# Threshold attention with a feed-forward block: fewer weight conversions in the first slots, w_ch2 by 128 output columns, diagonals on ScalarE

## The chip, the core and the metric

The kernel runs on one core of a Trainium2 chip. The core has five engines that run their own instruction streams in order: TensorE (PE, matrix products; PEld are its weight loads), VectorE (DVE), ScalarE (ACT), GpSimd (POOL) and SyncE (SP, which here only issues transfers). They meet through semaphores. The metric is the device time of one execution in microseconds: before the change 1488.72 us, the median of three runs (1486.18 to 1491.72).

## The reference, cut to what matters

Attention keeps, in each row of scores, only those within tau of the row's maximum. Its output, with the heads side by side, goes through a normalised two-layer block with a residual.

```python
# q, k, v: (8, 8, 576, 64) float32, tau = 0.02
scores = np.matmul(q, k.transpose(0, 1, 3, 2)) / 8
thresh = np.max(scores, axis=-1, keepdims=True) - tau
scores = np.where(scores >= thresh, scores, -1e9)
attn = np.exp(scores - np.max(scores, axis=-1, keepdims=True))
attn = attn / (np.sum(attn, axis=-1, keepdims=True) + 1e-9)
x = np.matmul(attn, v).transpose(0, 2, 1, 3).reshape(8, 576, 512)

xn = (x - mean(x)) / np.sqrt(var(x) + 1e-6) * g_ln          # over the last axis
out = x + np.maximum(xn @ w_ch1, 0) @ w_ch2                 # 512x2048, 2048x512
```

The two weight matrices arrive as 64-bit floats, 8 MB each. [...]the kernel turns their bits into float32 itself.

## The kernel before, in words

**Slots.** The 8 batches have 8 heads each; a unit is one pair of heads of one batch. For each batch the kernel runs nine slots: four with the first 256 query rows of each unit, one (s = 4) that gathers what the blocks of 32 rows leave over of all four units, and four with the next 256 rows. A slot makes 2304 columns of scores (L359, or L344 in the fifth slot), takes each row's maximum (`neg`, L372, two instructions on DVE), exponentials on ACT (`e`, L383, four), and the threshold with the row sum (L390, four on DVE, then a reciprocal, L394). There is one set of score banks: the next slot's scores wait until L390 of this slot has read them. A unit's q and k must have been turned by DVE (`kT` L304, `qT` L313, `q_diag` L316) after POOL has scaled q (L301); the buffers of q and k are single, so the loads of the next unit (L112) wait for those transposes.

**Turning the attention weights.** In the first batch PE does it: `tp` and `tr` (L100, L443) multiply the weights by a diagonal matrix that holds the reciprocals, so that turning and dividing are one product. The diagonals (`diag`, L404, four a slot) are made by POOL from an identity. ACT copies `tp` to `em` (L437) and `tr` to `rest` (L452), and the products with v (`pv`, L511) run in the next slot. From the second batch on POOL divides and a transpose on DVE and a trip through DRAM turn the weights.

**Feed-forward.** After the fifth and the ninth slot of a batch 288 rows of x are complete (a group g). POOL adds the four parts of x (`sum`, L537), PE averages over the features (`mean`, L546), DVE centres (`xc`, L552), and `ffn_steps` (L605) hands out the products one by one: sixteen blocks `p1` over w_ch1, each with a ReLU copy into `hidden` on ACT (L622), then four blocks `p2` over w_ch2, each of sixteen products. `second_part` (L675) puts some of these products into each quarter of a slot, as many as a pace (`owed`) asks for, so that PE has work while the softmax chain runs. `ready` (L668) gives the quarter in which a group starts: 24 (slot 6) for the first, 41 for the second. PE's order is thus fixed when the program is written out; the engines then only wait for each other. `ps_ff` has two PSUM buffers, shared by `tp`, `tr`, `mean`, `p1` and `p2`.

**Weights.** The class `Weights` (L160) brings the 16 chunks of w_ch1 and 16 of w_ch2 in, 128 partitions by 512 numbers each. A chunk takes raw space and, while it is converted, made space; both come from a list of pieces (`free`) in memory that is not in use yet: parts of `w2_sb`, of `hidden`, of the buffer `et`, and `stage`. A tick does up to three things, for three different chunks: `end` (L260: DVE L266 finishes the number and, for w_ch1, POOL L271 multiplies by g_ln), `carry` (L253: an integer add on POOL, L257), `begin` (L229: L239 and L243 on DVE, L247 and L251 on ACT). Which ticks a slot has stands in the main loop:

```python
ticks = range(1, 4 + n // 3) if n < 6 else range(6)
```

so three in slots 0 to 2, four in slots 3 to 5, six from slot 6 on. `fetch` (L209) issues loads of further chunks on SP's queue. A chunk of w_ch2 is 128 rows by all 512 columns, so that the first block `p2`, which needs all 2048 rows, needs all sixteen chunks; `ffn_steps` hands out no product whose chunk isn't converted in program order (L639).

Of the kernel before, what the change touches and what calls it, by code (L numbers as in the profile page):

```python
# [8 lines left out]
F32 = mybir.dt.float32  # L9
U32 = mybir.dt.uint32  # L10
I32 = mybir.dt.int32
I64 = mybir.dt.int64
# [6 lines left out]
def kernel(  # L19
# [31 lines left out]
    nc = tc.nc  # L51
    B, H, S, D = q.shape
    DM = H * D
# [3 lines left out]
    NK = DM // 128  # L57
    ND = DF // 128
    J = 4
    NB = S // 32  # L60
    TOK = S // 2
# [7 lines left out]
    consts = ctx.enter_context(tc.tile_pool(name="consts", bufs=1))  # L69
# [4 lines left out]
    ffn = ctx.enter_context(tc.tile_pool(name="ffn", bufs=2))  # L74
# [8 lines left out]
    ident = consts.tile([128, 128], F32, name="ident")  # L83
    avg_sb = consts.tile([128, 128], F32, name="avg_sb")
    w1_sb = [consts.tile([128, DF], F32, name=f"w1_{i}") for i in range(NK)]
    w2_sb = consts.tile([128, ND, DM], F32, name="w2")
    q_diag = [consts.tile([128, 128], F32, name=f"q_diag{i}") for i in range(HP)]
    rests = [consts.tile([128, 4, 128], F32, name=f"rest{i}") for i in range(2)]
    v_rest = [consts.tile([128, 2, D], F32, name=f"v_rest{i}") for i in range(HP)]
    hidden = consts.tile([128, ND, TOK], F32, name="hidden")  # L90
# [11 lines left out]
    def load_qk(u, engines=None):  # L102


        b, hp = units[u]
        tiles = []
        for i, (name, src) in enumerate((("q", q), ("k", k))):
            t = ins.tile([128, NB, 32], F32, tag=name, bufs=1, name=f"{name}_in")
            for h in range(2):
                for e in range(2):  # L110
                    g = 2 * h + e
                    (engines[i] if engines else nc.sync).dma_start(  # L112
                        out=t[32 * g : 32 * g + 32],
                        in_=src[b, 2 * hp + h, :, 32 * e : 32 * e + 32].rearrange(
                            "(n r) c -> r n c", r=32
                        ),
                    )
            tiles.append(t)
        loaded[u] = tuple(tiles)

    def load_v(u):
# [13 lines left out]
        out=tau_sb, in_=bass.AP(tensor=tau.tensor, offset=tau.offset, ap=[[0, 128], [1, 1]])  # L135
    )
    load_qk(0, (nc.sync, nc.scalar))
    for t in q_diag + rests + v_rest:
# [21 lines left out]
    class Weights:  # L160
# [12 lines left out]
        def __init__(self):  # L173
            self.chunks = [
                (w1_sb[i][:, c : c + WC], w_ch1[i * 128 : (i + 1) * 128, c : c + WC], i)
                for c in range(0, DF, WC)
                for i in range(NK)
            ] + [(w2_sb[:, i], w_ch2[i * 128 : (i + 1) * 128, :], None) for i in range(ND)]
            self.n1 = NK * (DF // WC)
            self.fetched = self.begun = self.carried = self.ended = 0  # L180
            self.raw, self.made, self.due, self.ticks = {}, {}, [], 2
            flat = lambda t: t.rearrange("p a b -> p (a b)")
            stage = consts.tile([128, 8, WC], F32, name="stage")
            et = att.tile([128, NB, 128], F32, tag="et", bufs=1, name="et0")

            n1 = self.n1
            self.free = []  # L190
            for t, n, before in (
                (w2_sb, ND // 2, lambda p: n1 + 2 * p),
                (hidden, 4, lambda p: 10),
                (et, 2, lambda p: 2 * n1),
                (stage, 4, lambda p: 2 * n1),
            ):
                for p in range(n):
                    self.free.append((before(p), -1, flat(t)[:, p * 2 * WC : (p + 1) * 2 * WC]))
# [10 lines left out]
        def fetch(self, most=99):  # L209

            while self.fetched < len(self.chunks) and most:
                i = self.fetched
                if sum(p[0] > i for p in self.free) <= 2:
                    break
                got = self.piece(i, 1)
                if got is None:
                    break
                most -= 1
                self.fetched += 1
                self.raw[i] = got  # L220
                nc.sync.dma_start(out=got[2].bitcast(I64), in_=self.chunks[i][1])

        def give(self, got):
            self.free.append((got[0], self.ticks, got[2]))
# [160 lines left out]
    def weights(es, thr, divide):  # L385


        den = small.tile([128, 4], F32, tag="den", name="den")
        for i in range(4):
            nc.vector.scalar_tensor_tensor(  # L390
                out=es[:, i], in0=blocks[i], scalar=thr[:, i : i + 1], in1=es[:, i],
                op0=ALU.is_ge, op1=ALU.mult, accum_out=den[:, i : i + 1],
            )
        nc.vector.reciprocal(den, den)  # L394
        diags = []
        for i in range(4):
            if divide:
                src = dst = es[:, i]
            else:
                if i % 2 == 0:  # L400
                    two = ffn.tile([128, TOK], F32, tag="o", bufs=6, name="diag")
                src, dst = ident, two[:, i % 2 * 128 : i % 2 * 128 + 128]
                diags.append(dst)
            nc.gpsimd.tensor_scalar(  # L404
                out=dst, in0=src, scalar1=den[:, i : i + 1], scalar2=1.0,
                op0=ALU.mult, op1=ALU.mult,
            )
        return diags
# [196 lines left out]
    def ffn_steps(g):  # L605

        xc = centred.pop(g)
        rb = None  # L610
        for d in range(ND):
            while conversion.ended < 4 * (d // 4 + 1):
                yield 0
            p1 = ps_ff.tile([128, TOK], F32, tag="ff", name="p1")
            for c in range(NK):
                product(
                    p1, lhsT=w1_sb[c][:, d * 128 : (d + 1) * 128], rhs=xc[:, c],
                    start=(c == 0), stop=(c == NK - 1),
                )
                if c < NK - 1:  # L620
                    yield 1
            nc.scalar.activation(hidden[:, d], p1, func=AF.Relu)  # L622
            yield 2
            if d == 1:
                sq = ffn.tile([128, NK, TOK], F32, tag="sq", bufs=1, name="sq")
                nc.scalar.activation(sq, xc, func=AF.Square)  # L626
                for c in range(1, NK):
                    nc.gpsimd.tensor_tensor(out=sq[:, 0], in0=sq[:, 0], in1=sq[:, c], op=ALU.add)  # L628
            if d == 8:
                var = ps_ff.tile([128, TOK], F32, tag="ff", name="var")  # L630
                product(var, lhsT=avg_sb, rhs=sq[:, 0], start=True, stop=True)
# [72 lines left out]

    conversion = Weights()
    if w_ch1.dtype == I64:
        conversion.fetch(5)
    else:
        for i in range(NK):
            nc.sync.dma_start(out=w1_sb[i], in_=w_ch1[i * 128 : (i + 1) * 128])  # L710
            nc.scalar.mul(w1_sb[i], w1_sb[i], g_sb[:, i : i + 1])
        for i in range(ND):
            nc.sync.dma_start(out=w2_sb[:, i], in_=w_ch2[i * 128 : (i + 1) * 128])
        conversion.begun = conversion.carried = conversion.ended = len(conversion.chunks)

    turn(0)
    load_qk(1)
    load_v(1)
    for n in range(NS):
        b, s = divmod(n, SLOTS)  # L720
        ticks = range(1, 4 + n // 3) if n < 6 else range(6)

        def tick(i):
            if i in ticks:
# [6 lines left out]
        es, thr = next(rest)  # L731
# [85 lines left out]
```

## Time and profile before

| | |
|---|---|
| time | 1488.72 us (1486.18 to 1491.72) |
| profiled span | 1486.6 us |
| PE busy | 1418.2 us, 95% |
| DVE busy | 875.1 us, 59% |
| POOL busy | 476.1 us, 32% |
| ACT busy | 402.5 us, 27% |
| products of the feed-forward (L100, `p`) | 515.0 + 513.9 us |
| scores (L359) | 159.7 us |
| diagonals and divisions (L404) | 186.5 us for the divisions of the later batches; 27.4 us for 36 diagonals |
| moved by DMA | 205 MB, 138 GB/s on average |

A row of the profile's timeline reads: start, duration, engine, line of the kernel, operation, what is written and read, shapes, how many were merged, and in brackets how long the engine was idle before and what released it. The busy tenths cut the span into forty equal slices, one digit each; PEclk is the clock that PE was granted, in tenths of its full speed. Busy time on PE is modelled, and covers matmuls that run at a low clock too, so a longer row for the same matmuls is lost time as well. A buffer's number is left out of its name: `w` stands for all parts of the weights, and memory that is lent to the conversion shows under the name of its owner (`hidden`, `et`, `stage`).

### The profile page before, as it was taken

What the parts mean: (1) busy time and instruction counts of PE and PEld (TensorE: products, weight loads), DVE (VectorE), ACT (ScalarE), POOL (GpSimd) and SP (SyncE); (2) the same over time, 40 slices, a digit from 0 to 9 for tenths busy, and PEclk for the clock granted to TensorE, in tenths of its full rate; (3) what the DMA queues carried; (4) which work ended last, traced back from release to release, by engine and by line L of the source; (5) the groups of instructions that cost most, each with busy time, mean ns of one, the idle gap of its engine ahead of it and who ended that gap; (6) DMA issues with size and microseconds to landing.
All of it is one profiled execution on the core that took longest, in us unless ns stands there. A gap on an engine that the chain in (4) does not pass through costs nothing.

```text
span 1486.6 us, 29712 instructions
## 1 busy us (share of the span) xinstructions
PE 1418.2 (95%) x12168; PEld 875.2 (59%) x12168; DVE 875.1 (59%) x1524; ACT 402.5 (27%) x766; POOL 476.1 (32%) x737
## 2 busy tenths in 40 slices
PE   4858989999999999999999999999999999999998
PEld 2646655565556555665556555665556655565654
DVE  5877737656664566556665566556665566655211
ACT  3655413222221222223131222213132221312020
POOL 3785323232332233232332323222332323332100
PEclk8879999999999999999999999999999999999999
DMA  9612237565865577455874587556775558555301
GB/s 227 169 57 89 58 87 146 144 165 135 180 158 140 135 170 169 132 145 141 184 170 132 132 168 180 141 140 152 165 165 143 146 130 186 156 140 126 90 9 16
DMA packets 460695, 205.12 MB, mean 138 GB/s; under 512 B 275024, under 2 KB 420176, under 8 KB 460560
## 3 DMA queue, kind: packets, MB, share of 16 engines
q1 hardware_dynamic: 458160, 202.93, 56.7%
q8 instruction: 95, 1.56, 0.4%
q10 hardware_dynamic: 2368, 0.30, 0.2%
q14 instruction: 40, 0.33, 0.1%
q0 software_dynamic: 32, 0.00, 0.0%
HBM read 119.41 MB, written 83.76 MB: 137 GB/s over the span
## 4 chain that ended last, share of the span: by engine, by line
PE 81%; DMA 5%; SPq 4%; DVE 4%; ACT 2%; POOL 2%; issue 1%; POOLq 0%; DVEq 0%; ACTq 0%
PE p L100 60%; PE sc L511 9%; PE sc L359 9%; DMA em<-scr 2%; SPq L112 2%; PE sc L100 2%; ACT e L383 1%; DVE e L390 1%; SPq L475 1%; DMA rest<-scr 1%; DMA scr<-et 1%; POOL diag L404 1%; PE tr L443 1%; PE mean L100 1%; DVE neg L372 1%
## 5 line engine op out<-in xcount | busy, mean ns | idle before, releaser
L100 PE MATMUL p<-xc,w 128*64 128x288 f32 x4096 | 515.0, 407 | 2.7 <-ACT hidden L622 1.9
L100 PE MATMUL p<-hidden,w 128*64 128x288 f32 x4096 | 513.9, 407 | 0.2 <-ACT rest L452 0.2
L100 PEld LDWEIGHTS p<-xc,w 128*64 128x64 f32 x4096 | 299.0, 137 | 195.2 <-ACT hidden L622 7.7
L100 PEld LDWEIGHTS p<-hidden,w 128*64 128x64 f32 x4096 | 300.2, 137 | 188.7 <-ACT rest L452 0.7
L372 DVE TENSOR_REDUCE neg<-sc 128x2 f32<-128x1152 f32 x144 | 189.4, 1352 | 261.7 <-PE sc L359 235.3
L383 ACT ACTIVATE e<-sc,neg 128x576 f32<-128x576 f32 x288 | 194.7, 742 | 316.9 <-DVE neg L372 316.8
L404 POOL TENSOR_SCALAR e<-e,den 128x576 f32<-128x576 f32 x252 | 186.5, 758 | 252.9 <-DVE den L394 252.9
L390 DVE SCALAR_TENSOR_TENSOR e<-sc,thr,e 128x576 f32<-128x576 f32 x288 | 219.6, 812 | 36.8 <-ACT e L383 36.2
L469 DVE STREAM_TRANSPOSE et<-e 128x1152 f32<-128x1152 f32 x112 | 153.4, 1375 | 76.2 <-POOL e L404 58.6
L622 ACT ACTIVATE hidden<-p 128x288 f32<-128x288 f32 x256 | 105.9, 414 | 302.2 <-PE p L100 301.2
L359 PE MATMUL sc<-kT,qT 64*128 64x64 f32 (+3 forms) x1024 | 159.7, 445 | 26.9 <-DVE e L390 16.8
L376 POOL TENSOR_SCALAR thr<-neg,low_sb 128x2 f32<-128x2 f32 x144 | 42.7, 297 | 375.0 <-DVE neg L372 370.0
L359 PEld LDWEIGHTS sc<-kT,qT 64*128 64x128 f32 x1024 | 88.8, 194 | 113.3 <-issue 81.6
L511 PE MATMUL sc<-em,v_in 128*64 128x256 f32 (+1 forms) x1408 | 131.4, 330 | 6.9 <-DMA em<-scr 3.5
L511 PEld LDWEIGHTS sc<-em,v_in 128*64 128x64 f32 x1408 | 88.1, 137 | 45.7 <-DVE et L469 9.8
L528 ACT COPY x<-sc 128x256 f32<-128x256 f32 x60 | 22.4, 373 | 308.5 <-PE sc L511 305.0
L569 DVE TENSOR_TENSOR o<-p,rb 128x288 f32<-128x288 f32 x64 | 28.5, 445 | 130.1 <-PE p L100 130.1
L570 POOL TENSOR_TENSOR o<-o,x 128x288 f32<-128x288 f32 x64 | 51.0, 797 | 129.2 <-DVE o L569 127.3
L537 POOL TENSOR_TENSOR sum<-sum,x 128x256 f32<-128x256 f32 (+1 forms) x64 | 31.9, 498 | 84.2 <-ACT x L528 81.7
L628 POOL TENSOR_TENSOR sq<-sq 128x288 f32<-128x288 f32 x48 | 38.7, 806 | 40.4 <-ACT sq L626 37.9
L511 PE MATMUL sc<-rest,v_rest 128*64 128x256 f32 (+1 forms) x352 | 44.8, 329 | 0.0
L537 POOL TENSOR_TENSOR sum<-x 128x256 f32<-128x256 f32 (+1 forms) x32 | 16.3, 508 | 72.4 <-ACT x L528 43.8
(111 smaller groups left out, 774.7 us busy)
## 6 DMA issues: line engine op xcount, KB each, us to landing
scr<-et SPq DMA_DIRECT2D x252, 288.0 KB, 4.6
em<-scr SPq DMA_DIRECT2D x63, 1024.0 KB, 5.9
q_in<-in_q_dram SPq DMA_DIRECT2D x128, 72.0 KB, 3.7
out_dram<-ot SPq DMA_DIRECT2D x256, 36.0 KB, 4.2
k_in<-in_k_dram SPq DMA_DIRECT2D x124, 72.0 KB, 2.7
v_in<-in_v_dram SPq DMA_DIRECT2D x64, 128.0 KB, 4.2
rest<-scr SPq DMA_DIRECT2D x63, 128.0 KB, 5.9
w<-in_moe_w_ch_dram SPq DMA_DIRECT2D x12, 512.0 KB, 4.8
```

The lines of the kernel that those rows point to most:

```text
L100: nc.tensor.matmul(out[r], lhsT=lhsT[:, r], rhs=rhs, **flags)
L359: nc.tensor.matmul(sc[h][:, at : at + n], lhsT=qT[r, half, j * 128 : (j + 1) * 128], rhs=kT[r, o : o + n], start=True, stop=True,)
L372: nc.vector.tensor_reduce(out=neg[:, i], in_=sc[h][:, : 2 * S].rearrange("p (j n) -> p j n", j=2), axis=AXL.X, op=ALU.max, negate=True,)
L376: nc.gpsimd.tensor_scalar(out=thr[:, i], in0=neg[:, i], scalar1=-1.0, scalar2=low_sb, op0=ALU.mult, op1=ALU.add,)
L383: nc.scalar.activation(es[:, i], blocks[i], func=AF.Exp, bias=neg[:, i : i + 1])
L390: nc.vector.scalar_tensor_tensor(out=es[:, i], in0=blocks[i], scalar=thr[:, i : i + 1], in1=es[:, i], op0=ALU.is_ge, op1=ALU.mult, accum_o ...
L404: nc.gpsimd.tensor_scalar(out=dst, in0=src, scalar1=den[:, i : i + 1], scalar2=1.0, op0=ALU.mult, op1=ALU.mult,)
L469: nc.vector.transpose(et[:, :, 64 * h : 64 * h + 64].rearrange("p n (j c) -> p j n c", j=2), es[:, 2 * h : 2 * h + 2].rearrange("p j (n c) ...
L511: nc.tensor.matmul(dst[64 * h : 64 * h + 64], lhsT=vt[:, c, h, :] if c < J else vr[:, h, :], rhs=pick(em[:, c] if c < J else er, hp, h), s ...
L537: nc.gpsimd.tensor_tensor(out=sums[g][:, cols], in0=x[:, 0, cols] if c == 1 else sums[g][:, cols], in1=x[:, c, cols], op=ALU.add,)
L570: nc.gpsimd.tensor_tensor(out=o, in0=o, in1=groups[g][:, m], op=ALU.add)
L622: nc.scalar.activation(hidden[:, d], p1, func=AF.Relu)
```

## The change

It does six things.

- The ticks of slots 0 to 2 go from three to two, and of slots 3 to 5 from four to three. Six conversions move behind slot 5, where the slots have six ticks as before.
- w_ch2 is kept as `w2_sb[128, 4, 16, 128]`, by blocks of 128 output columns. A chunk is four blocks of 128 rows by 128 columns, and the first block `p2` needs the first four chunks only, the second the next four, and so on. It is meant to let the deferred conversions arrive in time.
- The diagonals of the first batch are made by ScalarE (`nc.scalar.mul`, identity times reciprocal) and no longer by POOL.
- The q and k of the second unit are issued by ACT's queue, and no longer stand on SP's queue behind the first weight chunks. Four chunks are fetched first, not five.
- The first group starts at quarter 25 and the second at 42, one later each: its mean and centring move into slot 6 (10), behind the first `tp` products.
- The third buffer of `x`, not in use before the second batch, is lent to the conversion as one more piece (`x_room`).

```diff
-    w2_sb = consts.tile([128, ND, DM], F32, name="w2")
+    w2_sb = consts.tile([128, NK, ND, 128], F32, name="w2")
...
-            ] + [(w2_sb[:, i], w_ch2[i * 128 : (i + 1) * 128, :], None) for i in range(ND)]
+            ] + [
+                (
+                    w2_sb[:, m, d : d + 4].rearrange("p d c -> p (d c)"),
+                    w_ch2[d * 128 : (d + 4) * 128, m * 128 : (m + 1) * 128].rearrange(
+                        "(d p) c -> p d c", p=128
+                    ),
+                    None,
+                )
+                for m in range(NK)
+                for d in range(0, ND, 4)
+            ]
...
+            x_room = ffn.tile([128, NK, TOK], F32, tag="x", bufs=3, name="x_room")
...
+                (x_room, 1, lambda p: 2 * n1),
...
-            if divide:
-                src = dst = es[:, i]
-            else:
+            if not divide:
                 if i % 2 == 0:
                     two = ffn.tile([128, TOK], F32, tag="o", bufs=6, name="diag")
-                src, dst = ident, two[:, i % 2 * 128 : i % 2 * 128 + 128]
-                diags.append(dst)
+                diags.append(two[:, i % 2 * 128 : i % 2 * 128 + 128])
+                nc.scalar.mul(diags[i], ident, den[:, i : i + 1])
+                continue
             nc.gpsimd.tensor_scalar(
-                out=dst, in0=src, scalar1=den[:, i : i + 1], scalar2=1.0,
+                out=es[:, i], in0=es[:, i], scalar1=den[:, i : i + 1], scalar2=1.0,
...
-                while conversion.ended < conversion.n1 + d + 1:
+                while conversion.ended <= conversion.n1 + 4 * m + d // 4:
                     yield 0
                 product(
-                    p2, lhsT=w2_sb[:, d, m * 128 : (m + 1) * 128], rhs=hidden[:, d],
+                    p2, lhsT=w2_sb[:, m, d], rhs=hidden[:, d],
...
-            return (24, 41)[g]
+            return (25, 42)[g]
...
-        conversion.fetch(5)
+        conversion.fetch(4)
...
-    load_qk(1)
+    load_qk(1, (nc.scalar, nc.scalar))
...
-        ticks = range(1, 4 + n // 3) if n < 6 else range(6)
+        ticks = range(1, 3 + n // 3) if n < 6 else range(6)
```

More of the change, by code (lines that the diff above doesn't have):

```diff
@@ L191, in __init__ @@
             for t, n, before in (
-                (w2_sb, ND // 2, lambda p: n1 + 2 * p),
+                (w2_sb.rearrange("p m d c -> p (m d) c"), ND // 2, lambda p: n1 + 2 * p),
                 (hidden, 4, lambda p: 10),
                 (et, 2, lambda p: 2 * n1),
+                (x_room, 1, lambda p: 2 * n1),
                 (stage, 4, lambda p: 2 * n1),
@@ L220, in fetch @@
                 self.raw[i] = got
-                nc.sync.dma_start(out=got[2].bitcast(I64), in_=self.chunks[i][1])
+                _, src, gi = self.chunks[i]
+                raw = got[2].bitcast(I64)
+                nc.sync.dma_start(
+                    out=raw if gi is not None else raw.rearrange("p (d c) -> p d c", d=4), in_=src
+                )
         def give(self, got):
@@ L712 @@
         for i in range(ND):
-            nc.sync.dma_start(out=w2_sb[:, i], in_=w_ch2[i * 128 : (i + 1) * 128])
+            nc.sync.dma_start(
+                out=w2_sb[:, :, i],
+                in_=w_ch2[i * 128 : (i + 1) * 128, :].rearrange("p (m c) -> p m c", m=NK),
+            )
         conversion.begun = conversion.carried = conversion.ended = len(conversion.chunks)
     turn(0)
-    load_qk(1)
+    load_qk(1, (nc.scalar, nc.scalar))
     load_v(1)
```

## The prediction

> **What bounds the kernel now.** I read the busy tenths by slice first, then stretches, then the timelines of PE, VectorE (DVE) and GpSimd (POOL) over the first 220 us, then waits.
>
> ```profile
> PE   4858989999999999999999999999999999999998
> POOL 3785323232332233232332323222332323332100
> PEclk8879999999999999999999999999999999999999
> ```
>
> A slice is 37 us. PE is short of work, and its clock below full, only in the first four or five. The stretch from 200 us on says the rest is PE's own work:
>
> ```profile
> 200.00:1480.00 1280.00, 1271.52 (x10790) 766.71 (x10786) 732.42 (x1273) 303.98 (x590) 365.38 (x595) 1.00 0.60 142
> ```
>
> Columns: PE, weight loads, DVE, ACT, POOL busy, clock, DMA share, GB/s. PE is idle 8.5 us of 1280, at full clock; whatever comes off the start comes off the end. Summing PE over ten-microsecond stretches up to 200 gives 146.3 us busy, 53.7 idle. A slot is one unit of scores; its first row maximum on DVE (`neg`) marks it:
>
> ```profile
> 60.39 2.62 DVE L372 TENSOR_REDUCE neg<-sc 128x2 f32<-128x1152 f32 x2 [0.43 <-PE sc L359]
> ...
> 77.32 1.20 DVE L266 SCALAR_TENSOR_TENSOR hidden<-hidden 128x512 f32<-128x512 f32 x1 [2.19 <-POOL hidden L257]
> 78.44 0.41 DVE L239 TENSOR_SCALAR w<-stage 128x512 uint32<-128x512 uint32 x1
> 78.89 0.98 DVE L243 SCALAR_TENSOR_TENSOR w<-stage,w 128x512 uint32<-128x512 uint32 x1
> 79.79 2.61 DVE L372 TENSOR_REDUCE neg<-sc 128x2 f32<-128x1152 f32 x2
> ...
> 96.92 2.61 DVE L372 TENSOR_REDUCE neg<-sc 128x2 f32<-128x1152 f32 x2
> ...
> 120.04 2.61 DVE L372 TENSOR_REDUCE neg<-sc 128x2 f32<-128x1152 f32 x2
> ```
>
> Slots 0 to 6 mark at 13.86, 30.88, 44.61, 60.39, 79.79, 96.92, 120.04: pitches 17.0, 13.7, 15.8, 19.4, 17.1, 23.1. At 77 us a weight conversion stands ahead of `neg` on DVE, and waits 2.19 us for POOL, which held the diagonals:
>
> ```profile
> 71.84 3.53 POOL L404 TENSOR_SCALAR diag<-ident,den 128x128 f32<-128x128 f32 x4 [3.61 <-DVE den L394]
> 75.34 0.69 POOL L271 TENSOR_SCALAR w<-w,g_sb 128x512 f32<-128x512 f32 x1
> 76.00 1.28 POOL L257 TENSOR_TENSOR hidden<-hidden,et 128x512 int32<-128x512 int32 x1
> ```
>
> PE pays twice, in gaps and in slow matmuls after them:
>
> ```profile
> 54.87 5.89 PE L359 MATMUL sc<-kT,qT 64*128 64x512 f32 x16 [3.74 <-DVE e L390]
> ...
> 88.92 2.33 PE L359 MATMUL sc<-kT,qT 64*128 64x512 f32 x16
> ...
> 112.44 1.23 PE L100 MATMUL mean<-sum,avg_sb 128*64 128x288 f32 x4 [6.27 <-POOL sum L537]
> ...
> 123.33 0.98 PE L443 MATMUL tr<-diag,e 128*64 128x128 f32 x7 [2.63 <-ACT em L437]
> ```
>
> The same 16 score matmuls take 2.33 us, or 5.89 after a 3.74 us gap.
>
> **What the Trainium skill says.** "TensorE: Matmul & The Clock Gate", Part 1: PE falls to half clock after an idle window of about 3.4 us and needs as much busy time to return. The trace agrees: slow after gaps of 3.74, 5.45, 6.27 us, full after 2.63. "SBUF — State Buffer", Who interferes with whom: a DVE instruction with two SBUF inputs contends with a GpSimd one that reads SBUF. L266 and L243 are such, and take 0.66 to 1.2 and 0.69 to 1.8 us. "DMA: Bandwidth & Descriptors", Issuing engines are not separate DMA queues: another issuing engine saves issue time, not bandwidth; the DMA share is 0.94 to 1.15 from 0 to 20 us, so there is none spare. Price: "ScalarE: Activation LUTs", What ACT_TABLE_LOAD costs: with a per-partition pointer 280 ns + 0.833 ns an element; for 576 that is 760, and L383 measures 742.
>
> **The change, part by part.** One conversion costs DVE 0.66 + 0.42 + 0.69 = 1.8 us alone, near 2.1 beside POOL; POOL 1.3, for w_ch1 0.7 more; ACT 1.35.
>
> *One conversion fewer in each of slots 0 to 5* (9 + 12 = 21 become 6 + 9 = 15), and *diagonals on ACT*. POOL loses 3.5 + 2 us a slot: its waits on the path (2.19 before `neg`, 2.14 before a `qT` at 50.0) go. On ACT four diagonals cost between 4 x 0.27 (its 128x128 copy, L519) and 4 x 0.39 less overlap (the price): 1.1 to 1.3, I take 1.2. They stand between conversions, after the exponentials, before the next slot's `em` copies; `em` of the next slot needs its scores first, so about 0.5 us shows. Rebuilding a slot from its rows, T being `neg`:
> - Slot 1: `neg` 2.65, turn 2.0, half a conversion 1.2; the last two exponentials end at T+7.5 (as now), so `e` ends T+8.7; scores 2.3: pitch 11.1.
> - Slot 2: `neg` 2.65, turn 2.0 with 0.3 for `q_in`, conversion 2.0, `e` 3.0 to T+10; scores 2.3, over the other conversion: 12.6.
> - Slots 3 and 4, no turn: `e` ends T+9 (exponentials, 1 us wait as now), then two conversions 3.9: 12.9 each. Scores at full clock end inside that.
> - Slot 5 with slot 6's first: three conversions: 15.
>
> PE has 9.8 us in such a slot (scores 2.33, `tp` 3.85, `tr` 0.98, `pv` 2.65), with gaps of 2.0 (`pv` ends T+7.1, scores start T+9.1) to 2.2 us (round the mean, below): under the 2.63 that left it at full clock, so I take full clock.
>
> *Second unit on ACT's queue.* Now its eight loads stand on SyncE behind five weight chunks, issued 10.33 to 18.3, and DVE waits:
>
> ```profile
> 21.02 0.78 DVE L304 STREAM_TRANSPOSE kT<-k_in 128x576 f32<-128x576 f32 x1 [4.54 <-DMA k_in<-in_k_dram]
> ```
>
> ACT issued four such in 2.07 us, so eight end at 14.4 if they start at 10.33. They wait for unit 0's transposes, and behind them stand ACT's table load (1.28) and the first exponentials, which need scores at 15.2 anyway: 0.5 us later, hidden, since `e` starts only at 23.9. `kT` lands between 16.5 (DVE free) and 21.0: I take 18.0, so slot 1 at 27.9. Four chunks first instead of five helps it.
>
> *Mean one quarter later.* It no longer stalls PE 6.3 us ahead of slot 6's scores, but stands between `tp` pairs, and takes one of two PSUM buffers until DVE has centred, after `neg`. With ACT's `em` copies at 14.7 after slot 5's mark, mean to 15.9, `neg` to 17.5, centre to 19.1, `tp` and `tr`: the first w_ch1 product (`p`) starts at 21.3.
>
> Sum: 27.9 + 11.1 + 12.6 + 12.9 + 12.9 = 77.4 for slot 5, + 21.3 = 98.7. Now `p` starts at 124.04. From there PE holds a queue of products and is 93 to 100% busy to 190 us, so 25.3 us come off.
>
> *Six deferred conversions.* Slots 6 to 8 now hold 6, 6, 5. DVE: slot 8 then has 2.65 + 2.0 + 3.0 + 10 = 17.7 us, PE 9.8 + 54 products of 0.25 = 23.3: hidden. w_ch2 by output columns asks for four chunks per block of 128 instead of all sixteen, so the pause at the last product of the first block, before slot 9, goes; it cost little, since other blocks followed. Chunks land as 1 KB runs rather than 4 KB, off the path. The extra x buffer is free memory; the weight's row stride is not a cost the trace shows. Net of all these: 0, with -3 to +6 for the range.
>
> Forecast: 1488.7 - 25.3 + 0.6 for contention = 1464.
>
> **The rivals.**
> - *A, half the gain* (0.17): the second unit lands no sooner, and slots 1 to 5 lose only the DVE share of a conversion, 5 x 1.9, plus 2.5 of mean's stall: 12 us, 1476.7. For it: gaps moved by ACT's order could reach 3.7 us and halve the clock. Against: POOL's waits are measured and vanish.
> - *B, more* (0.08): slot 1 at 26.9, pitches 11.1, 12.3, 12.4, 12.4, `p` 20 on: 95, so 29, and half of the 6 us idle left between 124 and 200: 1456.7. For it: less port contention. Against: deferred conversions raise it again there.
> - *C, no gain or slower* (0.13): A's 12 us are given back by six deferred conversions at 2 us each where slot 8's products wait for them, and two restarts at half clock cost 3.5 each: 1495.7. For it: all four engines have more to do in slots 7 and 8. Against: DVE was idle 2.58 and 4.97 us around slot 8, and PE's order has 14 us of products in it.
>
> **How the numbers follow.** My forecast 0.62. Lowest: B's 1456.7 with the -3 of deferred conversions; highest: A with 2 more: 1454 to 1479 leaves C and tails out. Faster by 0.5% is below 1481.3: forecast, A and B, 0.87; C is split 0.07 same, 0.06 slower.
>
> **What would show it.** Right: marks near 28, 39, 52, 65, 77; no slow scores after slot 1; POOL never ahead of `neg`; `p` from about 99; `kT` of unit 1 near 18. Wrong: gaps over 3 us on PE between slots 1 and 5, scores of 5 us there, exponentials later than T+7.5 because of ACT's diagonals, or PE waiting for L283 (the conversion's last DVE step) in slots 8 and 9.

## The result, and the profile after

The changed kernel takes 1480.75 us (median of 4 runs, 1478.69 to 1483.58) beside 1489.39 us of the kernel before (a fourth run has joined the three behind the 1488.72): ratio 0.9945, interval 0.9919 to 0.9971. Measured once more beside other kernels (e9 below) the ratio is 0.9944, 0.9930 to 0.9957. So it is faster, by 8 us and not by 25. The profiled spans are 1479.8 and 1486.6 us.

The busy tenths of the changed kernel, slices of 37 us:

```profile
PE   2878999999999999999999999999999999999998
PEclk9999999999999999999999999999999999999999
```

The third and sixth slices are fuller (7 for 5, 9 for 8), but the first has fallen from 4 to 2: the start got worse before it got better. The 9 of TensorE's clock row in the first slice is no gain: a second profile of the same kernel (e9) has a 7 there, and the scores in this slice are slow in both (5.74 and 5.70 us for what takes 2.33). The stretch from 200 us on, columns as in the prediction:

```profile
200.00:1480.00 1280.00, 1262.61 (x10711) 766.97 (x10707) 729.14 (x1265) 303.30 (x589) 362.38 (x590) 1.00 0.59 142
```

The kernel ends 6.8 us earlier: of the 17.4 us in which PE is not busy here, 6.4 lie behind its last matmul, and 11.0 are idle where the kernel before had 8.5. The steady part is as before; the whole story is in the first 220 us. VectorE's timeline there (start, duration, what it did, idle before it):

```profile
26.19 0.78 DVE L321 STREAM_TRANSPOSE kT<-k_in 128x576 f32<-128x576 f32 x1 [9.56 <-DMA k_in<-in_k_dram]
...
69.05 0.66 DVE L283 SCALAR_TENSOR_TENSOR hidden<-hidden 128x512 f32<-128x512 f32 x1
69.63 0.42 DVE L256 TENSOR_SCALAR w<-w 128x512 uint32<-128x512 uint32 x1
70.09 1.07 DVE L260 SCALAR_TENSOR_TENSOR w<-w 128x512 uint32<-128x512 uint32 x1
71.08 1.79 DVE L283 SCALAR_TENSOR_TENSOR hidden<-hidden 128x512 f32<-128x512 f32 x1
72.79 0.95 DVE L256 TENSOR_SCALAR hidden<-w 128x512 uint32<-128x512 uint32 x1
73.77 1.06 DVE L260 SCALAR_TENSOR_TENSOR hidden<-w,hidden 128x512 uint32<-128x512 uint32 x1
74.75 2.61 DVE L389 TENSOR_REDUCE neg<-sc 128x2 f32<-128x1152 f32 x2
```

Three things are to be seen. Unit 1's `kT` waits 9.56 us for `k_in` and comes at 26.19, where it came at 21.02 before and was predicted at 18.0. In slots 1 to 5 no conversion waits 2 us for GpSimd ahead of `neg` any more (the 2.19 of before is gone; in slot 6 there is such a wait, below). But the two conversions between 69.05 and 74.75 now take 5.7 us, 2.85 each, against the 1.8 that one takes alone. GpSimd's timeline in the same microseconds shows what lies beside them:

```profile
69.83 0.78 POOL L288 TENSOR_SCALAR w<-hidden,g_sb 128x512 f32<-128x512 f32 x1 [3.99 <-DVE hidden L283]
70.59 1.73 POOL L274 TENSOR_TENSOR hidden<-hidden,w 128x512 int32<-128x512 int32 x1
```

VectorE's last step L283 (L266 in the kernel before) grew from 0.66 to 1.79 just while GpSimd's add L274 ran, and the add grew too, from 1.29 to 1.73. After it GpSimd goes on with other work up to 76 us, and VectorE's next steps are slow as well. TensorE's timeline:

```profile
30.71 5.74 PE L376 MATMUL sc<-kT,qT 64*128 64x512 f32 x16 [16.73 <-DVE e L407]
...
102.27 0.71 PE L100 MATMUL mean<-sum,avg_sb 128*64 128x288 f32 x4 [1.59 <-POOL sum L553]
...
132.26 1.75 PE L459 MATMUL tr<-diag,e 128*64 128x128 f32 x7 [3.11 <-ACT em L453]
```

The scores of slot 1 come after a gap of 16.73 us; the stall of 6.27 us ahead of the mean is down to 1.59; products start at 108.24 (124.04 before); and in slot 7 a gap of 3.11 us, not there before in this size, brings `tr` to half speed (1.75 us for 0.98).

Marks of slots, first products and the end, all in us:

| | slot 1 | slot 2 | slot 3 | slot 4 | slot 5 | first product | end of the span |
|---|---|---|---|---|---|---|---|
| before | 30.88 | 44.61 | 60.39 | 79.79 | 96.92 | 124.04 | 1486.6 |
| predicted | 27.9 | 39.0 | 51.6 | 64.5 | 77.4 | 98.7 | - |
| changed | 36.23 | 47.55 | 59.79 | 74.75 | 88.50 | 108.24 | 1479.8 |

Of the 15.8 us by which products start sooner, 6.8 are left at the end. Nine are given back, nearly all in slots 6 to 8. With the matmuls of products already issued counted at 0.125 us each (64 of them took 7.97 us; a product is two), the changed kernel leads by 16 us at the scores of slot 7, by 12 at those of slot 8, by 9 at those of slot 9, and by 8 at those of slot 16. What TensorE loses is the gaps ahead of `tr` in slots 7 and 8, 3.11 and 2.63 us, and the slow matmuls after them. VectorE in slot 6, and TensorE's scores of slot 7:

```profile
119.20 1.17 DVE L283 SCALAR_TENSOR_TENSOR w<-w 128x512 f32<-128x512 f32 x1 [2.63 <-POOL w L274]
120.30 1.52 DVE L256 TENSOR_SCALAR et<-et 128x512 uint32<-128x512 uint32 x1
121.86 1.66 DVE L260 SCALAR_TENSOR_TENSOR et<-et 128x512 uint32<-128x512 uint32 x1
...
128.98 2.62 DVE L389 TENSOR_REDUCE neg<-sc 128x2 f32<-128x1152 f32 x2
```

```profile
122.71 2.33 PE L376 MATMUL sc<-kT,qT 64*128 64x512 f32 x16
```

Five conversions run here from 112.08 to 128.98, 16.9 us in all, 3.4 each; 2.63 of the 16.9 are the wait for GpSimd's add. The third finds all three of its steps stretched, the last two only L256, from 0.42 to 1.52 (124.05 and 126.81). Two steps of the second, 1.03 and 1.18, lie beside another work of GpSimd, the squares for the variance (L644, 113.92 to 117.24). Slot 7's `neg` comes at 128.98 although its scores ended at 125.04, and slot 8's at 159.64 with scores that ended at 156.16: VectorE, not TensorE, sets the pace in slots 6 to 8.

### The profile page after: what moved, and what is told of

It is laid out like the page before. It is cut to its first block, busy times and chain, and to the rows that moved or that the text cites. A ratio compares the mean times of both kernels' runs of the same rounds, so it can differ in the third digit from the quotient of the medians.

```text
span 1479.8 us, 29677 instructions
## 1 busy us (share of the span) xinstructions
PE 1412.3 (95%) x12168; PEld 877.5 (59%) x12168; DVE 881.5 (60%) x1524; ACT 411.9 (28%) x802; POOL 455.2 (31%) x701
## 4 chain that ended last, share of the span: by engine, by line
PE 71%; DMA 7%; SPq 6%; DVE 4%; issue 2%; POOL 1%; ACT 1%; POOLq 0%; DVEq 0%; ACTq 0%
PE p L100 52%; PE sc L527 9%; PE sc L376 7%; DMA em<-scr 4%; SPq L491 2%; DMA scr<-et 2%; PE sc L100 2%; SPq L112 1%; DMA rest<-scr 1%; SPq L126 1%; SPq L130 1%; DVE e L407 1%; POOL e L420 1%; DVE neg L389 1%; ACT e L400 1%
## 5 line engine op out<-in xcount | busy, mean ns | idle before, releaser
L100 PEld LDWEIGHTS p<-hidden,w 128*64 128x64 f32 x4096 | 307.3, 137 | 181.3
L376 PE MATMUL sc<-kT,qT 64*128 64x448 f32 (+3 forms) x1024 | 158.6, 439 | 28.2 <-DVE e L407 18.7
L544 ACT COPY x<-sc 128x256 f32<-128x256 f32 x60 | 22.3, 372 | 301.2 <-PE sc L527 299.3
L644 POOL TENSOR_TENSOR sq<-sq 128x288 f32<-128x288 f32 x48 | 39.1, 814 | 39.1 <-ACT sq L642 36.6
L100 PE MATMUL tp<-diag,e 128*64 128x128 f32 x576 | 35.6, 276 | 5.9 <-ACT em L453 5.6
```

What stands on the lines that cost most here:

```text
L100: nc.tensor.matmul(out[r], lhsT=lhsT[:, r], rhs=rhs, **flags)
L376: nc.tensor.matmul(sc[h][:, at : at + n], lhsT=qT[r, half, j * 128 : (j + 1) * 128], rhs=kT[r, o : o + n], start=True, stop=True,)
```

## The experiments

My theory after the result had two parts. First, the second unit's `k` lands later on ScalarE's queue, because it is issued late there and shares the DMA engines with weight chunks. Second, with the diagonals gone GpSimd starts its add right beside VectorE's conversion steps, and both slow down. Rivals: that slot 1 is late for another reason; that conversions are long of themselves; that everything won early is taken back by slots 6 to 8 in any case. Ratios are to the kernel before; the changed kernel has 0.9944. No run undoes the layout of w_ch2, the lent buffer of `x` or the first fetch of four chunks by itself, so what these three are worth stays open.

**e1: the second unit back on SyncE.**

```diff
-    load_qk(1, (nc.scalar, nc.scalar))
+    load_qk(1)
```

> The changed kernel with the second unit's q and k issued by SyncE again (four chunks first, as changed). Theory (the move to ACT's queue is what went wrong: the next weight chunks overtook k): unit 1's kT starts near 20 to 21 us instead of 26.2, the mark of slot 1 comes at 30 to 31 instead of 36.2, all later marks move with it, and the time falls by 5 to 6 us, to about 1475. Rival (the late start is absorbed by the slots behind it, and the loss sits in slots 6 to 8 alone): the time stays within 1.5 us of the changed kernel's 1480.8.

Measured: 0.9893 (0.9877 to 0.9908), 1476.0 us; `kT` at 19.91, slot 1 marked at 29.95, 6.3 us sooner. The theory's numbers hold: this edit of the change is a loss. Of the 6.3 us, 1.9 go at once into a longer slot 1 (13.2 us to the next mark for 11.3); the lead is 4.4 at slot 6 and 4.3 at the end.

**e2: only ScalarE's queue, in the kernel before.** The same line, the other way round.

> The kernel before with only the second unit's q and k moved to ACT's queue (five chunks first, as before). Theory (the move alone costs): kT of unit 1 goes from 21.0 to 25 to 27 us, the mark of slot 1 from 30.9 to 35 to 37, and the time rises by 4 to 6 us, to about 1494. Rival (the move is harmless or of use by itself, as the prediction had it, and hurts only with the other edits): the mark at 28 to 31 and no more time than before.

Measured: 1.0033 (1.0021 to 1.0044), 5 us slower; `kT` at 27.57, and every mark from slot 1 to 9 is 6.1 to 6.2 us later. The part alone does the same harm without the rest of the change.

**e3: the diagonals back on GpSimd.**

```diff
-                nc.scalar.mul(diags[i], ident, den[:, i : i + 1])
+                nc.gpsimd.tensor_scalar(
+                    out=diags[i], in0=ident, scalar1=den[:, i : i + 1], scalar2=1.0,
+                    op0=ALU.mult, op1=ALU.mult,
+                )
```

> The changed kernel with the diagonals of the first batch made by GpSimd again. Theory (POOL's 3.5 us in a slot were on the path): slots 2 to 5 become 1 to 3 us longer each, POOL stands ahead of neg or q_in again, and the time rises by 4 to 10 us. Rival (with two and three conversions POOL has room enough, and ACT gains as much as POOL loses): slots within 0.5 us, time within 2 us of the changed kernel's.

Measured: 0.9975 (0.9962 to 0.9988), 4.6 us slower than the changed kernel. The sum was as expected and the place was not: the pitches into slots 4 and 5 are 12.75 and 12.9, *shorter* than the 15.0 and 13.75 of the changed kernel and just what the prediction had; the loss is in slots 5 to 7. VectorE and GpSimd of this kernel:

```profile
71.80 0.66 DVE L283 SCALAR_TENSOR_TENSOR hidden<-hidden 128x512 f32<-128x512 f32 x1
72.38 0.42 DVE L256 TENSOR_SCALAR w<-w 128x512 uint32<-128x512 uint32 x1
72.84 0.72 DVE L260 SCALAR_TENSOR_TENSOR w<-w 128x512 uint32<-128x512 uint32 x1
```

```profile
72.07 3.54 POOL L418 TENSOR_SCALAR diag<-ident,den 128x128 f32<-128x128 f32 x4 [2.64 <-DVE den L411]
...
76.24 1.29 POOL L274 TENSOR_TENSOR hidden<-hidden,w 128x512 int32<-128x512 int32 x1
```

With the diagonals at the head of GpSimd's queue the add comes at 76.24, when VectorE's two conversions are over, and these take 1.8 us each. The four small diagonals don't slow VectorE; it is GpSimd that pays, 3.54 us for four where another slot of this kernel has 2.48. The diagonals act as a shield. Their cost shows where a slot has more to do: slot 6 is marked 18.5 us after slot 5 (14.7 in the changed kernel).

**e4: slot 0's two weight chunks behind the second unit's loads,** ScalarE's queue kept.

```diff
-        conversion.fetch(2)
+        if n:
+            conversion.fetch(2)
         run_all(stores)
...
                 load_qk(u + 1)
+        if n == 0:
+            conversion.fetch(2)
         run_all(aside)
```

> The changed kernel, second unit on ACT's queue, but the two weight chunks that SyncE issued at 18.4 us come behind the loads of the third unit (which wait for unit 1's transposes), so none is in flight beside unit 1's k. Theory (k was late because the weights shared the transfer engines with it): k lands about 2.7 us after its last issue at 19.8, kT at 22 to 23 instead of 26.2, slot 1 at 32 to 33, 3 to 4 us off the time. Rival (k was late because ACT could not issue it before 17.8 and small packets on this queue are slow by themselves): kT stays at 25 to 26.5, the time unchanged within 1.5 us, or longer since the chunks come late.

Measured: 0.9894 (0.9880 to 0.9908), slot 1 marked at 31.67, 4.6 us sooner.

```profile
22.32 0.78 DVE L321 STREAM_TRANSPOSE kT<-k_in 128x576 f32<-128x576 f32 x1 [5.75 <-DMA k_in<-in_k_dram]
```

`k` was issued at 17.89, as late as in the changed kernel, and yet landed 3.9 us sooner. So of the late `kT`, about 4 us came from the chunks in flight beside it. The rest goes with the late issue: in e1 SyncE issued `k` from 13.54 on.

**e5: GpSimd's two steps of a conversion left out** (the weights lack the add of the low word and g_ln).

```diff
-            nc.gpsimd.tensor_tensor(out=ai, in0=ai, in1=self.words(i, I32)[:, :, 0], op=ALU.add)
...
-                out=dst if gi is None else a, in0=y, scalar=(1.0625 * 2.0**-15) ** 2, in1=a,
+                out=dst, in0=y, scalar=(1.0625 * 2.0**-15) ** 2, in1=a,
...
-            if gi is not None:
-                nc.gpsimd.tensor_scalar(
-                    out=dst, in0=a, scalar1=g_sb[:, gi : gi + 1], scalar2=1.0,
-                    op0=ALU.mult, op1=ALU.mult,
-                )
```

> The changed kernel with GpSimd's two steps of a weight conversion left out (the add of the two words, and for w_ch1 the multiplication by g_ln; VectorE's last step writes the weight straight to its place), so the weights aren't the reference's; every other instruction and every load stays. It tells whether VectorE's conversion steps are long because GpSimd works beside them. Theory (contention: with the diagonals gone from GpSimd, its add and multiplication now start together with VectorE's steps): a conversion on VectorE falls from 2.85 to about 1.9 us, slots 3 and 4 go from 15.0 and 13.75 to about 12.9, slots 6 to 8 give back 3 to 5 us less; first w_ch1 product near 104, ratio to the kernel before 0.988 to 0.991. Rival (the steps are long for another reason, such as ScalarE's or the DMA's traffic): pitches of slots 3 and 4 within 0.4 of 15.0 and 13.75, ratio 0.993 to 0.996.

Measured: 0.9831 (0.9812 to 0.9850), 17 us faster than the changed kernel, more than either theory had. VectorE:

```profile
71.42 0.69 DVE L282 SCALAR_TENSOR_TENSOR w<-hidden 128x512 f32<-128x512 f32 x1
72.02 0.42 DVE L256 TENSOR_SCALAR hidden<-w 128x512 uint32<-128x512 uint32 x1
72.48 0.69 DVE L260 SCALAR_TENSOR_TENSOR hidden<-w,hidden 128x512 uint32<-128x512 uint32 x1
...
119.83 2.62 DVE L383 TENSOR_REDUCE neg<-sc 128x2 f32<-128x1152 f32 x2 [2.93 <-PE sc L370]
```

The first three rows are the second conversion of slot 3, the same three instructions that took 3.7 us; with the one ahead of it 3.3 us instead of 5.7, and VectorE's own work is untouched. Slot 7 is marked at 119.83, and there `neg` waits 2.93 us for its scores: VectorE is no longer the bound. First product at 102.94, 5.3 us sooner; the end 16.4 us sooner. So two thirds of what GpSimd's steps cost shows only after the first product. In slots 7 and 8 TensorE's waits ahead of `tr`, 3.11 and 2.63 us in the changed kernel, are 0.28 and 0.24, and `tr` runs at full speed. The run takes GpSimd's time away as well as the contention, so 16 us is an upper bound for the latter, and no kernel that computes everything can have all of it.

**e6: the add ahead of the last step,** the same work in another order.

```diff
-            if self.ended < self.carried and self.due[self.ended] <= self.ticks:
-                self.end()
             if self.carried < self.begun:
                 self.carry()
+            if self.ended < self.carried and self.due[self.ended] <= self.ticks:
+                self.end()
```

> The changed kernel with the order inside a tick turned: GpSimd's add for the conversion begun a tick ago is issued ahead of the last step of the oldest one, so that it no longer stands behind GpSimd's multiplication by g_ln, which waits for VectorE. The work is the same. Theory (contention): the first add of a slot's two runs while VectorE waits for the exponentials (GpSimd was idle 3.99 us there), so less of it lies beside VectorE's conversion steps: slots 3 and 4 about 1 us shorter each, slots 6 to 8 1 to 2 us, ratio 0.991 to 0.993. Rival (it only moves the contention to VectorE's e steps or to the next tick): pitches within 0.4 us of the changed kernel's, ratio 0.994 to 0.996.

Measured: 0.9888 (0.9872 to 0.9904), 8 us faster than the changed kernel and more than the theory had, for two lines that change places. Pitches into slots 4 and 5 are 13.5 and 12.6; the two conversions take 4.3 us (5.7). GpSimd's first add starts before VectorE's steps do, in a gap in which it had stood idle 3.99 us.

**e7: the ticks of before,** three and four conversions a slot again.

```diff
-        ticks = range(1, 3 + n // 3) if n < 6 else range(6)
+        ticks = range(1, 4 + n // 3) if n < 6 else range(6)
```

> The changed kernel with the ticks of before: slots 0 to 5 start 3, 3, 3, 4, 4, 4 conversions and not 2, 2, 2, 3, 3, 3; all the rest of the change stays. Theory: one conversion costs a slot of 1 to 5 VectorE time of 2 to 2.9 us on the path, so the first w_ch1 product comes 9 to 12 us later, near 118; against that slots 6 to 8 hold fewer conversions and give back 5 to 8 us less; net +2 to +6, ratio 0.996 to 0.9985. Rival 1 (nothing is given back for the deferred conversions, as the prediction had it): +9 to +12, ratio 1.000 to 1.003. Rival 2 (all of it is given back): ratio 0.993 to 0.9955.

Measured: 1.0023 (1.0012 to 1.0033): 11.8 us slower than the changed kernel, and slower than the kernel before. My expectation fell. The number is that of rival 1, but not its reason: the first product comes 22.3 us later (130.5), and 8.2 us of that are won back by the end (span 1493.9), as the theory had it. What I mis-sized is a conversion in the early slots: the pitches grow by 1.9 to 6.2 us each, and in slots 4 and 5 TensorE's gaps pass 4.5 us, after which its matmuls are slow (a `tr` of 1.76 us, scores of 3.40 after it):

```profile
88.84 1.76 PE L459 MATMUL tr<-diag,e 128*64 128x128 f32 x7 [4.52 <-ACT em L453]
```

So the six deferred conversions are what makes the change faster; its other parts without them come to 3.4 us slower than before, and the move to ScalarE's queue alone cost 5 us in e2.

**e8: the mean and the products one quarter earlier again.**

```diff
-            return (25, 42)[g]
+            return (24, 41)[g]
```

> The changed kernel with the first two groups' mean and products one quarter earlier again, as before; all the rest stays. Theory (prediction's step on the mean): TensorE stalls 4 to 6 us for the sum ahead of slot 6's scores, which then also run at half clock; VectorE's centring comes earlier in exchange; slot 6's mark 3 to 6 us later, first w_ch1 product within 2 us of 108, end +1 to +4, ratio 0.995 to 0.997. Rival (VectorE bounds slots 6 to 8 anyway, so the stall is absorbed): ratio 0.994 to 0.995, lead lost at slot 6 back by slot 8.

Measured: 0.9934 (0.9915 to 0.9954), the same as the changed kernel. The stall is there, with its slow matmuls (1.23 us for four that take 0.71):

```profile
104.10 1.23 PE L100 MATMUL mean<-sum,avg_sb 128*64 128x288 f32 x4 [6.00 <-POOL sum L553]
```

The first product comes at 114.87, 6.6 us later, and at the end the intervals show nothing of it: the rival's number. Counted with the products issued, this kernel is 10 us behind the changed one at the scores of slot 6, 7 at slot 7, 4 at slot 8 and 2 at slot 9, while the marks stay 6 to 10 us late. The rival's reason, that VectorE bounds these slots, fits; that the products here stand a quarter earlier would also help, and no run parts the two. The stall was real and worth nothing that can be measured at the end.

**e9: the changed kernel again.** No edit.

> The changed kernel once more, unaltered, beside the next three on one chip, as the base they are compared with and to narrow its ratio. Theory: 0.9945 within its interval, 0.992 to 0.997.

Measured: 0.9944 (0.9930 to 0.9957), 1481.6 us.

**e10: g_ln's multiplication on ScalarE.**

```diff
-                nc.gpsimd.tensor_scalar(
-                    out=dst, in0=a, scalar1=g_sb[:, gi : gi + 1], scalar2=1.0,
-                    op0=ALU.mult, op1=ALU.mult,
-                )
+                nc.scalar.mul(dst, a, g_sb[:, gi : gi + 1])
```

> The changed kernel with one instruction moved: the multiplication of a converted w_ch1 chunk by g_ln goes from GpSimd to ScalarE; the rest stays, nothing is left out. Theory (contention between VectorE and GpSimd): 16 multiplications of 0.7 to 1.2 us leave GpSimd, the adds that stood behind them start earlier, and slots 3 and 4 lose 0.5 to 1.5 us each; ScalarE has room for 0.7 us a conversion after the exponentials; ratio 0.988 to 0.992. Rival (the multiplications now delay ScalarE's copies of the transposed weights and the conversion's ScalarE steps, on which the add waits): no better, ratio 0.994 or above.

Measured: 0.9910 (0.9890 to 0.9930), 5 us faster than e9. Pitches into slots 4 and 5 are 13.55 and 12.7 (15.0 and 13.7), and slot 3's two conversions take 4.0 us (5.7). That is what less contention would give, with nothing left out.

**e11: all mended,** the edits of e4, e6 and e10, with q on SyncE and k on ScalarE.

> The changed kernel with four things mended, nothing left out: the second unit's q on SyncE and its k on ScalarE's queue, slot 0's two weight chunks issued behind them, the add ahead of the last step inside a tick, g_ln's multiplication on ScalarE. Theory: kT of unit 1 at 17 to 20 and slot 1 marked at 28 to 30.5; the contention gone from slots 3 to 8; the gains of the weights behind k (5 to 7) and of the add ahead (5 to 8) partly overlap in slots 6 to 8: ratio 0.981 to 0.986. Rival (what slot 1 wins is taken back by slots 6 to 8, which VectorE bounds): no better than the best single mend, 0.987 to 0.989.

Measured: 0.9882 (0.9863 to 0.9902), no better than e6 alone: the rival's number, though the trace gives another reason. VectorE and SyncE's queue:

```profile
17.01 0.78 DVE L318 STREAM_TRANSPOSE kT<-k_in 128x576 f32<-128x576 f32 x1 [0.38 <-DMA k_in<-in_k_dram]
23.87 0.77 DVE L327 STREAM_TRANSPOSE qT<-q_in 128x256 f32<-128x256 f32 x2 [6.08 <-POOL q_in L315]
```

```profile
8.13 8.52 SPq L236 DMA_DIRECT2D hidden<-in_moe_w_ch_dram  x3
```

`k` was there at once; now `q` (issued at 16.75) stood behind weight chunks: SyncE was 8.52 us over three of them, and the list of waits puts 7.2 us of it down to the loads of `k_in`. Slot 1 came at 33.23. I had moved the wait from one operand to the other.

**e12: e11 with one conversion more in slot 5 and one fewer in slots 6 and 7.**

```diff
-        ticks = range(1, 3 + n // 3) if n < 6 else range(6)
+        ticks = range(1, (3, 3, 3, 4, 4, 5)[n]) if n < 6 else range(5 if n < 8 else 6)
```

> The kernel of the run before with one conversion more in slot 5 (four) and one fewer in slots 6 and 7 (five). Theory (with the contention gone a conversion costs VectorE about 2 us, so slots 6 and 7 are no longer bound by it): the conversion is paid in slot 5 and little comes back: within 1.5 us of the run before, or up to 2 slower. Rival (slots 6 and 7 are still bound by VectorE): 2 to 4 us faster.

Measured: 0.9871 (0.9852 to 0.9889). The intervals of e11 and e12 overlap; it tells nothing apart.

**e13: both causes away,** the edits of e5 and e1 (the weights lack the low word's add and g_ln).

> The changed kernel with GpSimd's two steps of a conversion left out (the weights aren't the reference's) and the second unit's q and k back on SyncE: both suspected causes away at once. Theory (these two are the whole shortfall): slot 1 marked near 30, pitches 11 to 13 to slot 5, first w_ch1 product near 96, time 1457 to 1464, ratio 0.977 to 0.9825. Rival (slots 6 to 8 take back what slot 1 wins, whatever the conversion costs): no better than 0.983 of the run without GpSimd's steps alone.

Measured: 0.9793 (0.9777 to 0.9810), 1460.4 us. Marks 29.87, 43.06, 54.98, 67.56, 79.06, first product at 97.39, where the prediction had 98.7. Against the kernel before it comes 26.7 us sooner, and the span ends 28.2 sooner (1458.4): with GpSimd's two steps away nothing is given back, and what slot 1 wins stays (5.0 us of span against e5). The rival falls. That 97.39 is so near 98.7 is in part luck: slot 1 and the pitch after it come 2 us later each than forecast, the pitch into slot 5 and the way from there to the first product are 1.4 and 3.0 us shorter.

**e14: nothing left out,** the edits of e1, e6 and e10.

> The changed kernel with three mends, nothing left out: second unit on SyncE, the add ahead of the last step inside a tick, g_ln's multiplication on ScalarE. Theory: slot 1 marked near 30 (3 us ahead of the kernel with four mends, where q stood behind weight chunks), first w_ch1 product near 102; of the 3 us some 1 to 2 are left at the end: ratio 0.985 to 0.988. Rival (VectorE bounds slots 6 to 8 still and takes all of it): 0.988 or above.

Measured: 0.9855 (0.9837 to 0.9873), 1469.7 us: 13 us faster than the changed kernel, and by its median the fastest that computes everything (e12's interval overlaps it). Slot 1 at 29.39, first product at 99.41. VectorE in slot 6:

```profile
109.74 1.77 DVE L283 SCALAR_TENSOR_TENSOR w<-w 128x512 f32<-128x512 f32 x1 [1.95 <-ACT w L264]
```

The step after it, L256, takes 1.51. The contention is mended in good part in slots 1 to 5 (pitches 11.3, 12.0, 13.6, 12.7; slot 3's two conversions take 4.0 us, 3.3 in e13) and hardly in slot 6: its five conversions take 15.7 us, 10.1 in e13. That is where most of the 9 us between e14 and e13 can lie; no run splits it from GpSimd's own time.

**e15: e14 with the ticks of e12.**

> The kernel of the run before with four conversions in slot 5 and five in slots 6 and 7. Theory (VectorE still bounds slots 6 and 7 in part): 1 to 3 us faster than it, ratio 0.983 to 0.987. Rival: the conversion in slot 5 costs as much as it saves, same within 1 us.

Measured: 0.9882 (0.9861 to 0.9903), 4 us slower than e14 by the ratios, whose intervals just overlap; both expectations missed. With a fourth conversion in slot 5 the mean waits 7.42 us behind ScalarE's `em` copies and the first product comes at 107.53, 8 us later; the two lighter slots win back half.

## Why the prediction was wrong

It forecast 1464 us, range 1454 to 1479; 1480.75 was measured. Two terms were mis-sized: when unit 1's `kT` comes (18.0 forecast, 26.19 measured), and what a conversion costs VectorE beside GpSimd (2.1 forecast, 2.85 to 3.4 measured). With the second fell the step that TensorE is the bound from the first product on. Point by point:

- **"Whatever comes off the start comes off the end."** True of e13 (26.7 and 28.2 us), not of the changed kernel (15.8 and 6.8). I took PE to be the bound from 124 us on; once products start at 108, slots 6 to 8 are bound by VectorE, and 9 of the 15.8 us are lost there.
- **"`kT` lands between 16.5 and 21.0: I take 18.0."** Failed, the largest term up to the first product: it came at 26.19, outside the bound, and slot 1 came 8.3 us late. The bound was wrong because I priced the issue and not the wait to issue. ScalarE issued four loads at 10.27, the next four at 17.83:

```profile
10.27 2.62 ACTq L112 DMA_DIRECT2D q_in<-in_q_dram  x4
17.83 1.99 ACTq L112 DMA_DIRECT2D k_in<-in_k_dram  x4
```

```profile
18.36 1.06 SPq L236 DMA_DIRECT2D w<-in_moe_w_ch_dram  x2
```

  Behind them the table load and the first exponentials moved to 19.85 and 21.14, and SyncE's next chunks, which the kernel before issued at 20.61, behind `k` on the same queue, were issued at 18.36 and ran beside it. The Trainium skill's "DMA: Bandwidth & Descriptors", Queues, rings and completion order, says that the DMA engines serve the queues in turn, and e4's 4 us agree. I had quoted its statement that a second issuing engine brings no bandwidth, and drawn only half the conclusion: here `k` was safe from the chunks issued after it while both were on one queue, and not on two. e1 and e2 show what the move costs, e4 what the chunks beside `k` do.
- **"Four diagonals on ACT: 1.2 us."** Right, 1.28. That POOL's waits ahead of `neg` go is right too, for slots 1 to 5.
- **"One conversion costs DVE 1.8 alone, near 2.1 beside POOL."** Failed: 2.85 in slots 3 and 4, 3.4 in slot 6. I carried the contention of before over to a schedule without the diagonals that had kept the two apart; in slots 3 and 4 a wait of 2 us went and contention of 2 us came. And the reading of "0.66 to 1.2" for L266 left out the longest. Slot 6 of the kernel before, one of the slots into which the six were to move, has

```profile
139.16 1.77 DVE L266 SCALAR_TENSOR_TENSOR w<-w 128x512 f32<-128x512 f32 x1 [2.23 <-POOL w L257]
```

  and four conversions there take 2.9 us each (131.82 to 136.84 and 139.16 to 145.66). The price lay in the trace. The skill's "SBUF — State Buffer", Who interferes with whom, which I used, also says that a VectorE instruction in a two-port mode and one of GpSimd shut each other out, the first to issue for its whole length, and that `tensor_scalar` (L256) can enter such a mode. The runs agree in size: L256 0.42 to 1.52, L283 0.66 to 1.79, each about 1.1 more beside an add that takes 1.29. They agree in time as well. Where the add started first, L283 ends 0.55 us behind the add's end in the changed kernel (72.32 and 72.87), 0.54 in e10 and 0.55 in e14, and L256 0.29 us behind it twice in slot 6, as if the step waited for the add and then ran. No run takes the mechanism apart further. That GpSimd's two steps cause the stretching is shown (e5); that their timing matters is what e3, e6 and e10 agree on.
- **The rebuilt slots.** 11.1, 12.6, 12.9, 12.9 were predicted, 11.3, 12.2, 15.0, 13.75 measured; e3 has 12.75 and 12.9 for the last two. Full clock in these slots is right; in slots 7 and 8 `tr` is slow (1.75 us) after gaps of 3.11 and 2.63 us, the second no longer than the gap that the prediction took for safe.
- **Mean one quarter later.** First product 19.7 us after slot 5's mark, 21.3 predicted. The size was about right, and nothing of it can be measured at the end (e8).
- **"Six deferred conversions: hidden, 0."** Failed in the changed kernel, by 9 us. The working priced 10 us for five conversions in slot 8; they take 16.9 in slot 6. At 10.1 (e13) they are hidden, as it said. So this step fell with the one on contention, and my range of +6 for it was short. Deferring still pays by itself: without it the kernel is 11.8 us slower (e7).
- **Rivals.** C named the deferred conversions and restarts at half clock (`tr`, 1.75 us), and what happened is the forecast's early gain, cut by 9.5 us, with C's giving back behind it. No case combined the two. A's 1476.7 comes near in number, and it had the second unit landing no sooner, but it had 12 us won early and kept, where 15.8 were won and 9 lost again. B's "less port contention" is the opposite of what came.

Sum to the first product: 8.3 (slot 1) + 2.9 (slots 3 and 4) + 0.2 - 0.4 - 1.6 (the rest) = 9.5, which is 108.24 - 98.7. With 9.0 given back that makes 18.5 between the predicted 25.3 and the 6.8 of the spans. e13 removes both causes and gives 1460.4, but with work left out; the best that computes everything, e14, is at 1469.7.

## What to carry to other kernels

When work leaves an engine, ask what moves up in its queue and what that then runs beside: a wait that you see in the profile may be keeping two engines apart. Before a load moves to another queue, look at what it stood in front of on the old one, and at when the new engine can issue it, with what stands behind it. And price an early gain at the place where it meets the next bound: a row's duration holds for its neighbours of now, not for those that it gets.

## What the runs showed of the hardware

- An engine can stand still between two loads that it issues: SyncE from 11.76 to 16.65 and ScalarE from 12.89 to 17.83 in the changed kernel, just while four weight chunks and unit 1's first loads were under way. The list of waits puts SyncE's 4.8 us down to the loads of `q_in`, and gives nothing for ScalarE's; what held them no run shows.
- The slow stretch of TensorE after a long gap is not of one length. After 16.73 us idle the scores took 5.74 us and the next 64 `tp` ran at once in 3.75; in e6, after 17.21 us, the scores took 5.89 and the 64 `tp` 5.89 too, which makes slot 2's pitch 13.2 for 11.3. This moves a mark by 2 us from one kernel to the next. The clock reading does not show the first of these: that profile has 1.00 from 18 to 40 us, where e9, the same kernel, has 0.50 from 20 to 30 and 0.65 from 30 to 40.
- A gap of 2.63 us left TensorE at full clock in the kernel before; in the changed kernel `tr` is slow (1.75 us) after a gap of 2.63 in slot 8, and full (0.98) after 2.54 in slot 7 of e9. The clock reading agrees for slot 8 (0.50 from 163 to 165 us). The gap alone doesn't tell.
